# Attention and feed-forward block on one Trainium2 core: a new table of positions for an attention unit, its products with the values in two stretches beside the turn of the maxima

## The chip, the cores and the metric

One core of one Trainium2 chip runs the whole program in one launch. The metric is device time in microseconds (us) of that launch. Beside it stands the span, the time from the first to the last instruction of one profiled execution. An engine is named as in the profile: PE is the matrix engine (TensorE), PEld its weight loads, DVE the vector engine, ACT the scalar engine, POOL is GpSimd, SP issues most of the transfers (DMAs).

## The reference

One layer over x with 2048 tokens of 512 values: a modulated layer norm, attention in 32 heads of 16 values in which each token sees itself and the 255 tokens before it, a second modulated layer norm, and a gated feed-forward of inner size 1792, both added to x.

```
mod = (silu(c) @ w_mod).reshape(1, 6, 1, 512); sa, ca, ga, sb, cb, gb = mod[:, 0..5]
h = layernorm(x) * (1 + ca) + sa
q, k, v = split((h @ wqkv), 32 heads of 16)
scores = where(0 <= i - j < 256, q @ k.T * 16**-0.5, -1e9)
x = x + ga * (softmax(scores) @ v @ wo)
h = layernorm(x) * (1 + cb) + sb
x = x + gb * ((silu(h @ w1) * (h @ w3)) @ w2)
```

## The kernel before, in words

The program has a prologue (modulation, layer norm, the values v of all tokens), an attention stage, and a feed-forward stage that begins while attention ends. The change is in the attention stage.

**Units.** Attention is cut into 32 units u, numbered by a group g of four heads and a block b of 512 tokens (u = 4g + b). A unit has three parts, written by three functions.

- `unit_a` (L442): twelve products `pj` (128x512, L451) make queries and keys of the unit from the normed tokens. ACT cuts the result out of PSUM into three tiles (L457 to L463), POOL takes two differences (`mix`, L469, about 1.29 us each), and SP sends three sets of rows (`rows`, L474, two DMAs each) into the big tile `ring`, where queries and keys of all tokens stand.
- `unit_b` (L491): sixteen products `mx` (L504, up to 128x384) give the scores with queries on the partitions. DVE takes the maximum of each (`top`, L511), joins the sixteen (`parts`, L519 and L520, tile `mr`), PE turns the little tile over (`turn`, L526), ACT cuts it out (`mT`, L531), and SP sends it as extra rows of the queries into `ring` (L535, two DMAs, one for each index a of 0 and 1). So a later product subtracts the maximum by itself.
- `unit_c` (L743): sixteen products `st` (L763) give the scores with keys on the partitions, indexed by a key block j of 0 to 3, by a, and by hh. Each covers the queries of up to three blocks of 128 tokens: for j = 2 and 3 the last of these lie in the next unit's block, so they read the rows that the next unit's turn has sent. A mask or a merge on DVE (L771, L781), the exponential on ACT (L775, L784, L800, L812) and a select on POOL (L791, L808) make the probabilities `pt`, of which nine tiles exist. Then `pv` (L735) multiplies them with the values into the one PSUM tile `po`: for each j four products of 17 columns, each in a 32-column part of the array. A unit's own four calls are for j = 0 to 3; two more are for j = 2 and 3 of the unit before it, whose keys reach into this block. At last ACT copies `po` out (`out`, L828) and SP stores it (L831).

PSUM holds three banks for `mx` and the turn, three for `st`, one for `pj`, one for `po`.

**What sets the order.** Every step is handed to `at` with a position, a number; the steps of all units are sorted by it and given out in that order, and each engine works through its own list in order. Unit u's part c starts at position 8u, its part b at 8(u-2) + ob, its part a at 8(u-3) + oa; the table `X` (L30) gives the offsets within a part. A unit is thus eight positions long, and three units are under way at once. From position 232 (`TS`, three units before the end) on, the steps keep their order, but a planner (`Sched`, L115) puts other work between them: first the projection with `wo` (L1120), then the second norm and the feed-forward. It works from modelled times, so a new table moves its choices too.

Of the kernel before, what the change touches and what calls it, by code (L numbers as in the profile page):

```python
# [26 lines left out]
NEG = -1e30  # L27
SCALE = DH ** -0.5

X = dict(oa=-1.228, ob=1.317, wqk=(-2.382, 3.131, 4.551), pj=(-1.966, -1.918, -1.881, -0.877, -0.359, -0.355,  # L30
         -0.265, 0.076, 1.497, 3.335, 3.917, 4.363), ev=(4.727, 5.775, 5.259), mix=(5.588, 6.021),
         row=(8.681, 8.806, 9.018), mx=(0.546, 0.669, 1.455, 2.0, 2.064, 2.307, 2.929, 2.957, 3.255, 4.081,
         4.688, 5.039, 6.139, 6.215, 6.787, 7.106), tl=(0.31, 0.576, 0.39, 0.716, 0.354, 0.742, 0.497, 1.151,
         0.762, 0.785, 0.491, 0.953, 0.338, 1.726, 1.317, 1.105), mr=(8.575, 8.773, 9.063, 9.269), st=(1.873,
         1.594, -2.503, 2.891, 0.05, 3.409, 2.644, 3.504, 4.618, 4.477, 4.419, 5.916, 5.311, 7.665, 6.691,
         6.671), c=(0.385, 0.805, 2.402, 0.573, 0.759, 1.126), pv=(4.115, 8.948, 9.091, 9.582, 3.792, 4.101),
         o=(9.93, 10.63), job=(-0.855, 2.493, 10.058))
Y = dict(wqk=(0, 4, 5), pj=(0.0, 0.382, 0.764, 1.146, 1.528, 1.91, 2.292, 2.674, 3.056, 3.438, 3.82, 4.202),
         ev=(4.991, 4.614, 4.813), mix=(5.389, 5.444), row=(5.416, 5.471, 6.776), mx=(0.0, 0.5, 1.0, 1.5,
         2.0, 2.5, 3.0, 3.5, 4.0, 4.5, 5.0, 5.5, 6.0, 6.5, 7.0, 7.5), tl=(0.402, 0.402, 0.402, 0.402, 0.402,  # L40
         0.402, 0.402, 0.402, 0.402, 0.402, 0.402, 0.402, 0.402, 0.402, 0.402, 0.402), mr=(8.402, 8.563,
         8.761, 9.49))
# [260 lines left out]
def block_kernel(ctx: ExitStack, tc: tile.TileContext, x, wqk, wv, wo, w13, w2, c, wmod, out):  # L303
# [137 lines left out]

    def unit_a(u, t0, at, y=X):  # L442

# [47 lines left out]
    def unit_b(u, t0, at, y=X):  # L491

        g, b = divmod(u, NB)
        v = {}

        def scores(i):
            qb, a, hh = i // 4, i // 2 % 2, i % 2
            gq = 4 * b + qb
            k0 = max(0, gq - 2)
            n = (gq + 1 - k0) * P  # L500
            if i == 0:
                v["mt"] = a1.tile([P, 2, 2, 4], F32, name="mt", bufs=2)
            v[i] = psA.tile([P, BT], F32, name="mx", bufs=MXB)
            nc.tensor.matmul(v[i][:, :n], queries(NS, a, gq, 1), keys(NS, hh, a, k0, gq + 1 - k0),  # L504
                             start=True, stop=True)
# [226 lines left out]

    held = {}

    def pv(kb, g, pts, qb, c0, nq, first, last):  # L735


        for i in range(4):
            nc.tensor.matmul(po[32 * i:32 * i + DH + 1, qb * P:(qb + nq) * P],  # L739
                             vS[:, kb, 4 * g + i], pts[i // 2][:, i % 2, c0:c0 + nq],  # L740
                             start=first, stop=last, skip_group_check=True)

    def unit_c(u, t0, at):  # L743

        g, b = divmod(u, NB)
        v = {}
# [68 lines left out]
        def values_of(j, uu):  # L815

            kb = 4 * (uu % NB) + j
            pts = [held[uu, j, a] for a in range(2)]
            nq = min(3, NT - kb)
            here = min(nq, 4 - j)  # L820
            if uu == u:
                pv(kb, g, pts, j, 0, here, b == 0 and j == 0, j == 3)
            elif nq > here:
                pv(kb, g, pts, 0, here, nq - here, j == 2, False)

        def out():
            v["os"] = a2.tile([P, BT], F32, name="os", bufs=1)
# [5 lines left out]
        for j in range(4):  # L833
            for a in range(2):
                m, c = mode(j, a), X["c"]
# [68 lines left out]
    for n in range(NU - 4):  # L904
        gate = 0 if n < 8 else 1
        if n >= 3 and n % 4 != 2 and gate == 0 and wog_left:
            i = wog_left.pop(0)
# [29 lines left out]
    last = [o for o in ops if o[0] >= TS]  # L937
# [557 lines left out]
    for b in range(NB):  # L1495
        at_ = us(8 * (NU - NB + b) + X["o"][1]) + 0.1
        o = sch.op("NIL", lambda: None, 0.0, 0.0, [], [("o_dr", b, NQ - 1)])
# [15 lines left out]
    for b in range(NB):  # L1513
        kb, ks = kb_[b], K["os"] + 0.1 * b
# [99 lines left out]
```

## Time and profile before

| | |
|---|---|
| median of three runs | 972.69 us (969.67 to 973.76) |
| span of the profiled execution | 971.3 us |
| PE busy in the span | 942.4 us (97%), 5316 instructions |
| DVE, ACT, POOL busy | 734.9 us (76%), 557.1 us (57%), 538.2 us (55%) |
| attention outputs `os` copied out | first at 109.9 us, last at 488.1 us |

The profile gives no time of its own for the profiled execution beside the span; the median of the runs is 1.4 us above that span. A line of the timeline has the start, the length, the engine, the line of the kernel, the operation, its tiles as out<-in, the shape, and in brackets how long the engine had been idle and what ended that. Matmuls overlap: the length of one is modelled to the end of its pass, and the next one starts before it. An idle time in brackets therefore counts only what lies beyond that modelled end.

### The profile page before, as it was taken

How to read it: one execution, taken by the hardware profiler on the slowest of the kernel's cores; microseconds unless marked ns; L12 is line 12 of the kernel's file. 1: busy time of each engine (PE TensorE's matmuls, PEld its weight loads, DVE VectorE, ACT ScalarE, POOL GpSimd, SP SyncE). 2: the span in 40 equal slices, each digit the busy share in tenths (PEclk: the TensorE clock that was granted, in tenths of full speed). 3: DMA queues.
4: the chain of work that ended last, by engine and by line, in shares of the span. 5: the costliest groups of instructions: out<-in, count | busy, mean ns of one | idle time of the engine just before them, and what ended most of it. 6: DMA issues, size and time to landing. Idle time of an engine off the chain costs nothing.

```text
span 971.3 us, 17150 instructions
## 1 busy us (share of the span) xinstructions
PE 942.4 (97%) x5316; PEld 717.5 (74%) x5316; DVE 734.9 (76%) x2034; ACT 557.1 (57%) x1258; POOL 538.2 (55%) x740
## 2 busy tenths in 40 slices
PE   6999999999999999998998999999999999999998
PEld 3678777777767776775577888888887888888886
DVE  7575889998989998999278686666679766677545
ACT  3333878787878787876578843433456343433330
POOL 8321777787868786865546765337759332222320
PEclk9999999999999999999898999999999999999999
DMA  9521354444544444435795564467654433222102
GB/s 317 170 77 36 134 182 143 144 143 144 176 143 143 144 144 143 133 128 174 211 243 139 194 217 151 142 206 249 194 195 165 141 119 94 63 65 72 44 23 87
DMA packets 80672, 141.65 MB, mean 146 GB/s; under 512 B 9538, under 2 KB 22338, under 8 KB 80580
## 3 DMA queue, kind: packets, MB, share of 16 engines
q1 hardware_dynamic: 79860, 139.50, 44.6%
q10 hardware_dynamic: 720, 1.05, 0.3%
q8 instruction: 42, 0.69, 0.3%
q14 instruction: 50, 0.41, 0.1%
HBM read 85.72 MB, written 34.61 MB: 124 GB/s over the span
## 4 chain that ended last, share of the span: by engine, by line
PE 83%; POOL 5%; DVE 4%; DMA 3%; issue 2%; ACT 2%; SPq 1%; POOLq 0%; DVEq 0%; ACTq 0%
PE st L1384 13%; PE mx L1384 11%; PE pj L451 7%; PE mx L504 7%; PE mx L1478 7%; PE st L763 7%; PE st L1478 7%; PE po L739 6%; PE pj L1384 5%; PE st L671 3%; PE pj L1478 2%; PE mx L1120 2%; POOL pt L791 2%; PE st L1120 2%; POOL qk L469 2%
## 5 line engine op out<-in xcount | busy, mean ns | idle before, releaser
L511 DVE CUSTOM_DVE_ANT_0 junk<-mx,mskq 128x384 bf16<-128x384 f32 (+2 forms) x512 | 256.3, 527 | 28.8 <-PE mx L504 27.2
L504 PE MATMUL mx<-ring 96*128 96x384 f32 (+2 forms) x512 | 154.9, 340 | 6.0 <-DMA ring<-qk 2.4
L763 PE MATMUL st<-ring 100*128 100x384 f32 (+2 forms) x512 | 155.3, 345 | 2.2 <-ACT pt L784 1.2
L791 POOL TENSOR_SCALAR_AFFINE_SELECT pt<-pt 128x256 f32<-128x256 f32 x268 | 109.3, 411 | 63.1 <-ACT pt L784 52.5
L451 PE MATMUL pj<-hT,wq 128*128 128x512 f32 x384 | 136.2, 404 | 1.2 <-DVE wq L440 0.8
L504 PEld LDWEIGHTS mx<-ring 96*128 96x128 f32 x512 | 93.5, 189 | 39.7 <-DVE mt L511 25.8
L784 ACT ACTIVATE pt<-st 128x256 f32<-128x256 f32 x268 | 96.1, 386 | 41.8 <-DVE st L781 33.8
L763 PEld LDWEIGHTS st<-ring 100*128 100x128 f32 x512 | 95.5, 190 | 23.7 <-issue 8.4
L739 PE MATMUL po<-pt,vS 128*17 128x384 f32 (+2 forms) x1408 | 98.6, 398 | 1.7 <-POOL pt L791 1.0
L469 POOL TENSOR_TENSOR qk<-qkr,qk 128x512 fp32r<-128x512 f32 x64 | 83.3, 1302 | 27.6 <-ACT qkr L457 27.4
L976 POOL TENSOR_TENSOR w<-w,w 128x512 fp32r<-128x512 f32 (+2 forms) x36 | 59.8, 1679 | 62.0 <-ACT w L975 44.6
L1428 POOL TENSOR_TENSOR t<-t,t 128x512 f32<-128x512 f32 x28 | 39.7, 1418 | 93.5 <-DVE t L1416 91.7
L781 DVE COPY_PREDICATED st<-later,st 128x128 f32<-128x128 uint8 x268 | 72.2, 291 | 17.4 <-PE st L763 14.5
L451 PEld LDWEIGHTS pj<-hT,wq 128*128 128x128 f32 x384 | 71.4, 190 | 10.2 <-issue 1.7
L739 PEld LDWEIGHTS po<-pt,vS 128*17 128x17 f32 x1408 | 33.5, 98 | 48.4 <-issue 22.4
L1384 PE MATMUL st<-b,w 128*128 128x512 f32 x258 | 64.1, 390 | 0.0
L775 ACT ACTIVATE pt<-st 128x384 f32<-128x384 f32 (+2 forms) x128 | 52.7, 434 | 18.8 <-DVE st L771 12.4
L1416 DVE TENSOR_TENSOR t<-st,t 128x512 f32<-128x512 f32 x52 | 35.7, 686 | 36.4 <-PE st L1384 31.2
L808 POOL TENSOR_SCALAR_AFFINE_SELECT sm<-sm 128x256 f32<-128x256 f32 x109 | 42.1, 409 | 27.9 <-ACT sm L798 25.2
L1456 ACT ACTIVATE wq<-g 128x512 fp32r<-128x512 f32 x28 | 17.8, 634 | 67.5 <-PE st L1478 40.7
L1384 PE MATMUL mx<-b,w 128*128 128x512 f32 x222 | 56.0, 390 | 0.0
L1384 PEld LDWEIGHTS st<-b,w 128*128 128x128 f32 x258 | 48.4, 188 | 10.2
(270 smaller groups left out, 2083.1 us busy)
## 6 DMA issues: line engine op xcount, KB each, us to landing
ring<-qk SPq DMA_DIRECT2D x192, 128.0 KB
o_dr<-os SPq DMA_DIRECT2D x32, 256.0 KB
w<-wsum SPq DMA_DIRECT2D x14, 512.0 KB
w<-w2g SPq DMA_DIRECT2D x14, 512.0 KB
jb<-in_w SPq DMA_DIRECT2D x24, 256.0 KB
wraw<-in_w SPq DMA_DIRECT2D x7, 768.0 KB
w<-wraw SPq DMA_DIRECT2D x14, 384.0 KB
vS<-in_wmod SPq DMA_DIRECT2D x20, 256.0 KB
```

Source lines behind the costliest of these rows:

```text
L451: nc.tensor.matmul(v["ps"], WQ[g][w][:, n // 3], hTp(i, n // 3, b * BT, BT), start=(n == 0), stop=(n == 3 * KC - 1))
L469: nc.gpsimd.tensor_tensor(out=v[n], in0=v["raw"], in1=v[1].bitcast(F32), op=ALU.subtract)
L504: nc.tensor.matmul(v[i][:, :n], queries(NS, a, gq, 1), keys(NS, hh, a, k0, gq + 1 - k0), start=True, stop=True)
L511: nc.vector.tensor_tensor_reduce(out=junk[:, :n], in0=v[i][:, :n], in1=mskq[:, 3 * P - n:], scale=1.0, scalar=-3e38, op0=ALU.add, op1=ALU. ...
L739: nc.tensor.matmul(po[32 * i:32 * i + DH + 1, qb * P:(qb + nq) * P], vS[:, kb, 4 * g + i], pts[i // 2][:, i % 2, c0:c0 + nq], start=first, ...
L763: nc.tensor.matmul(ps[:, :nq], keys(NM, hh, a, kb, 1), queries(NM, a, kb, nq), start=True, stop=not plus)
L781: nc.vector.copy_predicated(ps[:, 0], later, ps[:, 2])
L784: nc.scalar.activation(held[u, j, a][:, hh, :2], v[j, a, hh][:, :2], AF.Exp, scale=SCALE)
L791: nc.gpsimd.affine_select(out=pt[:, :, 2 * m], in_=pt[:, :, 0], **w)
L976: sch.op(eng, lambda: on_eng(eng).tensor_tensor(out=lo(), in0=src(), in1=hi().bitcast(F32), op=ALU.subtract), tt(eng, n), key, kl + kh, kl ...
L1384: nc.tensor.matmul(ps(bk), WT[s, n][w][:, col], BB[t, k][r], start=start and c == 0, stop=stop and c == 5, skip_group_check=True)
L1478: nc.tensor.matmul(ps(bk), tiles[hk + (h,)][:, i * P:(i + 1) * P], w2_of(last, y, f), start=(m == 0), stop=(m == 5))
```

## The change

The table `X` is replaced, which moves nearly every step of a unit. Two small edits let the order of steps change: the tile of maxima is made by whichever `mx` product comes first, and the first product with the values in a block, whichever it is, starts the sum in `po` (with `stop` always set).

```diff
@@ L30
-X = dict(oa=-1.228, ob=1.317, wqk=(-2.382, 3.131, 4.551), pj=(-1.966, -1.918, -1.881, -0.877, -0.359, -0.355,
-         -0.265, 0.076, 1.497, 3.335, 3.917, 4.363), ev=(4.727, 5.775, 5.259), mix=(5.588, 6.021),
-         row=(8.681, 8.806, 9.018), mx=(0.546, 0.669, 1.455, 2.0, 2.064, 2.307, 2.929, 2.957, 3.255, 4.081,
-         4.688, 5.039, 6.139, 6.215, 6.787, 7.106), tl=(0.31, 0.576, 0.39, 0.716, 0.354, 0.742, 0.497, 1.151,
-         0.762, 0.785, 0.491, 0.953, 0.338, 1.726, 1.317, 1.105), mr=(8.575, 8.773, 9.063, 9.269), st=(1.873,
-         1.594, -2.503, 2.891, 0.05, 3.409, 2.644, 3.504, 4.618, 4.477, 4.419, 5.916, 5.311, 7.665, 6.691,
-         6.671), c=(0.385, 0.805, 2.402, 0.573, 0.759, 1.126), pv=(4.115, 8.948, 9.091, 9.582, 3.792, 4.101),
-         o=(9.93, 10.63), job=(-0.855, 2.493, 10.058))
+X = dict(oa=-4.796, ob=-2.251, wqk=(1.186, 6.699, 8.119), pj=(-2.741, -2.421, -2.211, -1.547, -0.122, -0.074,
+         0.522, 1.025, 1.074, 2.472, 2.614, 2.671), ev=(2.692, 5.036, 4.238), mix=(5.574, 6.76), row=(6.587,
+         7.93, 8.329), mx=(4.257, 3.565, 1.99, 2.496, 1.136, 5.297, 5.616, 7.133, 3.18, 8.031, 1.491, 2.403,
+         6.488, 4.019, 2.272, 5.408), tl=(1.032, 0.638, 0.158, 0.51, 0.269, 0.803, 1.089, 0.704, 0.353, 1.162,
+         0.473, 0.456, 0.909, 0.376, 0.547, 1.073), mr=(9.863, 10.174, 10.231, 10.614), st=(-5.114, -3.184,
+         -1.405, -0.284, 1.27, -0.446, 0.145, 0.722, 4.856, 3.979, 1.375, 1.585, 2.957, 2.64, 3.771, 3.671),
+         c=(0.491, 1.492, 2.078, 0.51, 0.82, 3.255), pv=(2.043, 7.743, 8.008, 7.924, 2.306, 2.173), o=(9.93,
+         10.63), job=(-0.855, 2.493, 10.058))
@@ unit_b, scores
-            if i == 0:
+            if "mt" not in v:
                 v["mt"] = a1.tile([P, 2, 2, 4], F32, name="mt", bufs=2)
@@ pv
-    def pv(kb, g, pts, qb, c0, nq, first, last):
+    def pv(kb, g, pts, qb, c0, nq, first):
...
-                             start=first, stop=last, skip_group_check=True)
+                             start=first, stop=True, skip_group_check=True)
@@ unit_c, values_of
+            first = "pv" not in v
             if uu == u:
-                pv(kb, g, pts, j, 0, here, b == 0 and j == 0, j == 3)
+                v["pv"] = True
+                pv(kb, g, pts, j, 0, here, first)
             elif nq > here:
-                pv(kb, g, pts, 0, here, nq - here, j == 2, False)
+                v["pv"] = True
+                pv(kb, g, pts, 0, here, nq - here, first)
```

With the offsets added up, these are the positions in the frame of unit u (its part c starts at 0, the next unit's at 8):

| step | before | after |
|---|---|---|
| first stretch of products with the values | 3.79 (j = 2 of u-1), 4.10 (j = 3 of u-1), 4.12 (j = 0) | 2.04 (j = 0), 2.17 (j = 3 of u-1), 2.31 (j = 2 of u-1) |
| second stretch | 8.95 (j = 1), 9.09 (j = 2), 9.58 (j = 3) | 7.74 (j = 1), 7.92 (j = 3), 8.01 (j = 2) |
| `po` copied out by ACT | 9.93 | 9.93 |
| maxima of u+1: `parts`, turn, rows sent | 1.89, 2.09, 2.59 | -0.39, -0.08, 0.36 |
| first `st` of u that reads those rows (j = 2) | 4.42 | 1.38 |
| queries and keys of u+3: rows sent | 7.45, 7.58, 7.79 | 1.79, 3.13, 3.53 |
| first `mx` of u+3 | 9.86 | 6.89 |
| POOL's side job (`jb`, L880 or L889) | 2.49 | 2.49 |

On PE the turn stood by itself before, between an `mx` and a `pj` or `st`; after, it stands inside the second stretch, behind the products for j = 1. The lines of the kernel after lie up to three further down (the output copy is L831, the store L834, the projection with `wo` L1123).

## Prediction

> **What bounds the kernel now.** I read the page first, then the stretches, then PE's timeline of one unit, then what PE waits for.
>
> ```profile
> span 971.3 us, 17150 instructions
> PE 942.4 (97%) x5316; PEld 717.5 (74%) x5316; DVE 734.9 (76%) x2034; ACT 557.1 (57%) x1258; POOL 538.2 (55%) x740
> PEclk9999999999999999999898999999999999999999
> ```
>
> PE is busy for 97% of the span. The stretches of 50 us say the same of steady attention:
>
> ```profile
> 150.00:200.00 50.00, 49.64 (x371) 36.44 (x371) 46.36 (x196) 40.08 (x114) 39.24 (x73) 1.00 0.45 149
> 350.00:400.00 50.00, 47.87 (x362) 34.86 (x362) 44.10 (x190) 38.70 (x111) 36.01 (x65) 1.00 0.43 139
> ```
>
> The columns are PE, PEld, DVE, ACT, POOL busy, the granted clock, the DMA share and GB/s. PE is idle for 0.4 to 2.1 of 50 us, at full clock; DVE stands at about 90%, ACT at 80%. So a reordering can win only what PE loses between products, and lose as much as its new waits cost. How long a unit is, two copies of `po` say, 27 units apart:
>
> ```profile
> 122.38 0.60 ACT L828 ACTIVATE os<-po 128x512 f32<-128x512 f32 x1 [0.17 <-PE po L739]
> 444.55 0.60 ACT L828 ACTIVATE os<-po 128x512 f32<-128x512 f32 x1 [0.71 <-PE po L739]
> ```
>
> (444.55 - 122.38) / 27 = 11.93 us, so one of its eight positions is worth 1.49 us. Now PE inside one unit:
>
> ```profile
> 250.08 0.34 PE L504 MATMUL mx<-ring 96*128 96x384 f32 x1
> 250.35 1.62 PE L739 MATMUL po<-pt,vS 128*17 128x384 f32 x24
> 251.89 0.44 PE L763 MATMUL st<-ring 100*128 100x384 f32 x1
> 252.17 0.34 PE L504 MATMUL mx<-ring 96*128 96x384 f32 x1
> 252.35 0.34 PE L763 MATMUL st<-ring 100*128 100x384 f32 x1
> 252.53 0.34 PE L504 MATMUL mx<-ring 96*128 96x384 f32 x1
> 253.04 0.28 PE L526 MATMUL mx<-ident,mr 128*32 128x128 f32 x1 [0.18 <-DVE mr L520]
> 253.08 0.47 PE L451 MATMUL pj<-hT,wq 128*128 128x512 f32 x1
> 253.39 0.34 PE L763 MATMUL st<-ring 100*128 100x384 f32 x1
> 253.57 0.40 PE L451 MATMUL pj<-hT,wq 128*128 128x512 f32 x1
> 253.81 0.35 PE L504 MATMUL mx<-ring 96*128 96x384 f32 x1
> ...
> 255.09 0.34 PE L504 MATMUL mx<-ring 96*128 96x384 f32 x1
> 255.36 1.49 PE L739 MATMUL po<-pt,vS 128*17 128x128 f32 x24
> 256.78 0.62 PE L504 MATMUL mx<-ring 96*128 96x384 f32 x2
> 257.23 0.52 PE L763 MATMUL st<-ring 100*128 100x384 f32 x2
> ```
>
> Starts count here, not lengths. A 384-column product takes 0.175 us from start to start (252.17 to 252.35), a `pj` 0.235 (253.57 to 253.81). A product shown as 0.34 long thus hides 0.165 us: a wait shown as 0.18 idle cost 0.34 (252.53 to 253.04 is 0.51, less 0.175). A stretch costs something at its ends: 255.09 to 255.36 is 0.27, or 0.09 over the product; after it, 256.78 to 257.23 is 0.45 for two products, 0.10 over.
>
> **The change part by part.** Numbers and shapes of the attention products stay; two stretches a unit stay two. What changes is what stands beside what.
>
> *(1) The rows of queries and keys, sent earlier.* What PE waits for between 122 and 445 us:
>
> ```profile
> L504 PE MATMUL mx<-ring 96*128 96x384 f32 (+2 forms) x433 | 129.5, 340 | 3.7 <-DMA ring<-qk 2.0 <-DVE st L781 1.3 <-issue 0.2
> L526 PE MATMUL mx<-ident,mr 128*32 128x128 f32 x27 | 7.4, 276 | 0.9 <-DVE mr L520 0.9
> 374.66 0.41 PE L504 MATMUL mx<-ring 96*128 96x384 f32 x1 [1.82 <-DMA ring<-qk]
> ```
>
> The `mx` products have 3.7 us of idle time before them, in about six places, each the first `mx` of a unit (the last row is the largest). With the hidden 0.165 six times this is 4.7 us. Before, the last rows are due at 7.79 and the first `mx` at 9.86: 2.07 positions, 3.1 us. After, 3.53 and 6.89: 3.35 positions, 5.0 us. The largest wait, 1.8 us, is about covered by the 1.9 us gained. On SP the rows now stand behind the store of `os`, which waits for ACT's copy at 1.93, so some slack goes; I count **-4.7 us**, between 0 (a row set late behind that store) and -4.7.
>
> *(2) The turn waits less for `mr`.* The row of L526 has 0.9 us of idle in five places, with the hidden part 0.9 + 5 x 0.165 = 1.7 us. What makes `mr` late:
>
> ```profile
> 251.78 1.00 DVE L519 TENSOR_SCALAR mr<-mt 128x16 fp32r<-128x16 f32 x1
> 240.40 0.17 DVE L519 TENSOR_SCALAR mr<-mt 128x16 fp32r<-128x16 f32 x1
> 251.46 1.28 POOL L880 TENSOR_TENSOR jb<-jb,wqr 128x512 f32<-128x512 f32 x1
> ```
>
> L519 takes 0.17 us, but 1.00 where POOL's gating job (251.46 to 252.74) lies over it, and ends when that ends. After, `parts` is due at -0.39 (7.61 of the unit before) and the job stays at 2.49; POOL's next products, the mixes, come at 0.78. PE also has the j = 1 products between. I count **-1.7 us**, between -1.7 and, if a mix ran into `parts` in every unit, +0.34 x 30 = +10; I take the near end, since 1.2 positions (1.7 us) lie between.
>
> *(3) A drain behind a stretch goes.* 250.35 to 251.89 is 1.54 us for a stretch that an `st` follows; 255.36 to 256.78 is 1.42 for the same three groups with an `mx` behind. In the built program that `st` waits on PE's own semaphore, for `pt` tiles that the stretch frees; 25 `st` directly behind a stretch do so before, none after. 25 x 0.12: **-3.0 us** (0 if the freed tile is merely asked for later).
>
> *(4) The turn inside a stretch.* Alone, it cost little: 253.04 to 253.08 is 0.04, and the `pj` behind it 0.31, 0.08 over its 0.235; 0.12 in all, part of it its own pass. Inside, it uses the 32-column form that the products around it use. I count 0, between -0.12 x 30 = -3.6 and +3.6, and come back to it.
>
> *(5) The rows of the maxima, read sooner.* This is the added wait. Between the turn and the first `st` with j = 2, the built program has before: 257.23 - 253.04 = 4.19 us of PE's work. After: products for j = 3 and 2 (three blocks of 128; the stretch above has six in 1.42 less 0.12, so 0.65), leaving the stretch 0.12 + 0.10, three `pj` (0.71), and eight of `mx` and `st` (1.40), with the turn's 0.12: 3.10 us. Three quarters of the units have such an `st` (the last block of a group has none): 20 in the steady part. When do the rows land?
>
> ```profile
> 253.78 1.41 SPq L535 DMA_DIRECT2D ring<-mT  x2
> GB/s 0 0 0 0 131 0 0 0 0 0 0 0 0 0 0 0 12 53 0 0 0 0 25 41 0 229 393 344 426 360 328 164 131 98 98 344 410 393 426 345
> 313.73 0.27 PE L526 MATMUL mx<-ident,mr 128*32 128x128 f32 x1
> 317.76 0.30 PEld L763 LDWEIGHTS st<-ring 100*128 100x128 f32 x2 [0.24 <-DMA ring<-mT]
> ```
>
> The second row is the DMA rate from 253 to 258 us in slices of 0.125: the two little transfers, issued one behind the other, move in slices 17 and 18 and 23 and 24, so the second (a = 1, which the first `st` needs) has moved by 256.0, 2.96 us after the turn began at 253.04. The last two rows are the one place where an `st` was held by such rows: 317.76 - 313.73 = 4.03 us. Between 2.96 and 4.03 I take 3.35, nearer to the packets, since nowhere else did 4.19 fail. 3.35 - 3.10 = 0.25 us, 20 times: **+5.0 us**; from 0 to (4.03 - 3.10) x 20 = +19. Behind the waiting `st` on PE stand its neighbour, a `pj`, two `mx` and the first stretch; DVE's tops and ACT's exponentials of those wait with them, so the whole unit moves.
>
> *(6) `po` copied out closer to its next use.* Position 1.93 against a first product at 2.04 instead of 3.79. Now ACT comes early and waits (0.17 and 0.71 us in the rows of L828 above). After, the second stretch ends two positions before; ACT's queue ahead of the copy hides it or not. 0, at worst 0.60 x 30 = +18 if it lay open each time; near 0, as ACT has 10 of 50 us free.
>
> *(7) DVE, POOL and ACT work in another order.* Each keeps its instructions in a unit. DVE is the tightest:
>
> ```profile
> PEld mx L504 <- DVE mt L511: 21.4, 44, 0.6
> ```
>
> That is the wait for a free `mx` bank between 100 and 445 us: in weight loads, which run ahead; PE's own row of L504 names no such wait. After, three `mx` stand almost together behind the second stretch, but that stretch gives DVE 1.6 us to empty the banks. 0, between 0 and +21 if every such wait reached PE; near 0, as none does now. On POOL the two mixes (1.29 us each) now stand ahead of a unit's first masks; those are used more than four positions later.
>
> *(8) The tail.* From 445 us on the planner mixes in the projection with `wo`:
>
> ```profile
> 450.00:460.00 10.00, 8.19 (x46) 4.26 (x45) 9.46 (x28) 6.83 (x15) 3.66 (x6) 0.83 0.71 213
> 470.00:480.00 10.00, 8.72 (x66) 4.51 (x64) 2.49 (x7) 4.70 (x11) 6.38 (x9) 0.83 1.05 309
> 454.92 0.92 PE L504 MATMUL mx<-ring 96*128 96x384 f32 x2 [0.96 <-DVE mt L511]
> 455.76 2.75 PE L739 MATMUL po<-pt,vS 128*17 128x384 f32 x24
> 460.76 0.28 PE L526 MATMUL mx<-ident,mr 128*32 128x128 f32 x1 [1.34 <-DVE mr L520]
> ```
>
> PE waits 0.96 and 1.34 us for DVE here, and right behind a stretch takes 2.75 us instead of 1.62 at a clock of 0.83. After, parts a and b end 3.57 positions earlier against part c: fewer `mx` stand beside the last `st`, 48 instead of 24 projection products stand ahead of the last stretch, and the DVE work ahead of the last `parts` is shorter. The two waits and one slow stretch (2.3 + 1.1) may go; the last rows of maxima find less cover (two units, about 0.7 us each). 0.7 x 2 - 3.4 = **-2.0 us**, from -6 to +6.
>
> Sum: -4.7 - 1.7 - 3.0 + 5.0 - 2.0 = -6.4 us on the span of 971.3, so 964.9. The runs' median lies 1.4 us over the span: **966.3 us**.
>
> **The rivals.**
>
> *The rows of the maxima take the place of all that was won (slower).* At 4.03 us from turn to `st`, step 5 costs 19 and the sum is 971.3 - 9.4 + 19 - 2 = 978.9, with 1.4 about 980. Gain and loss without the tail meet at a wait of 9.4 / 20 = 0.47 us, a landing 3.57 us after the turn. For it: the job's 256 KB load now goes out just ahead of the rows, and ACT may be held when the turn ends. Against it: one such wait in 32 units before. Chance 0.22.
>
> *The tail gives it back (no change).* With fewer products to fill it, PE has more gaps there, and the clock falls again: 0.83 over 30 us costs 5.1 us. Without the 2.0 of step 8 that is 971.3 - 4.4 + 5.1 + 1.4 = 973.4, or 971 to 974 with a shorter dip. The Trainium skill, "TensorE: Matmul & The Clock Gate", part 1, says that the clock falls to half after an idle window of about 3.4 us and comes back after a busy one. The trace agrees in kind (2.75 us for a stretch at a clock of 0.83), but the idle time ahead of it, 0.96 us, is far shorter than that window. Chance 0.25.
>
> *Each entry to and exit from the 32-column form drains PE (faster still).* If the turn alone paid as a stretch does at its ends, 0.09 + 0.12 + 0.10 = 0.31 us, its place inside saves 30 x 0.31 = 9 us: 957. Against it stands the 0.12 of step 4. The Trainium skill, "TensorEngine Tiling (Array Packing)", Key Properties, says that changing the tiling mode drains the engine, which would make this the rule; the turn's own rows show a third of it. Chance 0.08.
>
> That the change does not do what it says is no case here: the built program has the turn behind the first four products of a second stretch in all units that the table places.
>
> **How the numbers follow.** My forecast, faster by about 6 us, has 0.45, with its own range 960 to 967.8; slower 0.22; no change 0.25; faster still 0.08. A measurement of this kernel can tell 0.5%, 4.9 us, from no change. So faster 0.45 + 0.08 = 0.53, same 0.25, slower 0.22. The range leaves out the ends of both outer cases: 956 to 980.
>
> **What would show it.** Right: hardly any idle of `mx` on `ring<-qk` left; the turn never behind `mr`; L519 always 0.17 us; stretch to next product 1.42 us throughout; new idle before `st` by `ring<-mT`, about 0.25 us in 20 units; units near 11.7 us. Wrong: `st` idle there of 0.5 us or more; first stretches behind ACT's copy; a granted clock under 0.83 between 440 and 490 us, or a last copy of `po` after 488 us.

## The result, and the profile after

| | before | after |
|---|---|---|
| median of the runs | 973.23 us (969.67 to 977.51) | 986.47 us (984.03 to 989.49) |
| span of the profiled execution | 971.3 us | 983.6 us |

The ratio is 1.0132, 95% interval 1.0096 to 1.0169: slower by 13 us, where 6 us faster was forecast. First the page of the changed kernel, in the same three lines.

```profile
span 983.6 us, 17203 instructions
...
PE 946.0 (96%) x5316; PEld 719.1 (73%) x5316; DVE 731.5 (74%) x2034; ACT 554.8 (56%) x1258; POOL 536.5 (55%) x740
...
PEclk9999999999999999999998999999999999999999
```

PE's busy time is 3.6 us longer, the span 12.3. So PE stands idle for about 9 us more, but the page does not say where. The copies of `po` that measured a unit before (ACT, now L831), and the last of them:

```profile
127.08 0.60 ACT L831 ACTIVATE os<-po 128x512 f32<-128x512 f32 x1
...
450.93 0.59 ACT L831 ACTIVATE os<-po 128x512 f32<-128x512 f32 x1
...
493.87 0.60 ACT L831 ACTIVATE os<-po 128x512 f32<-128x512 f32 x1 [3.34 <-PE po L739]
```

(450.93 - 127.08) / 27 = 11.99 us for 11.93. The first of these three copies is 4.7 us late (127.08 for 122.38) and the last of all 5.8 (493.87 for 488.1), but a copy is no fair mark any more: the new table does other work ahead of it. A fair mark is PE's work itself. I give every product of PE the median start-to-start time of its shape in the kernel before, add these up in order, and compare the moments at which the same sum is reached. The table shows how much later than before each kernel is (us); inside a unit the curve swings by 1.5 us either way, because the order differs.

| time in the kernel before, us | 99 | 158 | 215 | 335 | 395 | 468 | 503 | 525 | 560 | 577 | 654 | 738 | 960 |
|---|---|---|---|---|---|---|---|---|---|---|---|---|---|
| after | 0.0 | -1.0 | 2.7 | 2.8 | 2.5 | 2.5 | 4.1 | 8.7 | 7.8 | 9.6 | 9.4 | 12.5 | 12.5 |
| e1, new table to unit 27, then the old | 0.1 | -0.4 | 2.6 | 3.8 | 2.9 | 11.4 | 10.1 | 10.0 | 11.3 | 11.3 | 11.3 | 11.2 | 11.2 |
| e4, planner refitted | 1.1 | 0.6 | 4.1 | 3.4 | 2.7 | 3.1 | 0.2 | 1.8 | 1.7 | 1.7 | 1.8 | 2.1 | 1.8 |
| e9, one number of the planner | 0.8 | -0.2 | 2.7 | 2.8 | 2.0 | 1.1 | 2.1 | 2.4 | 3.3 | 3.3 | 3.3 | 3.3 | 3.3 |
| e13, old table, rows and job earlier | -0.1 | -0.7 | -0.8 | -3.9 | -5.2 | -7.4 | -6.0 | -5.5 | -5.4 | -5.4 | -5.4 | -5.4 | -5.4 |

Up to 468 us, all of steady attention, the change loses 2.5 us. The other 10 come behind it, while the planner mixes projection, second norm and feed-forward. What PE does there (timeline of the kernel after, then of before):

```profile
493.66 1.65 PE L1123 MATMUL st<-wo,x1b 128*128 128x512 f32 x6
497.15 8.78 PE L1123 MATMUL st<-wo,x1b 128*128 128x512 f32 x30 [1.84 <-ACT x1b L1103]
...
511.68 3.42 PE L1123 MATMUL mx<-wo,o 128*128 128x512 f32 x12 [1.44 <-DVE o L1106]
515.53 1.89 PE L1123 MATMUL mx<-wo,o 128*128 128x512 f32 x7 [0.43 <-DVE o L1106]
...
528.17 0.47 PE L1258 MATMUL st<-ident,wqr 128*128 128x128 f32 x1 [2.40 <-ACT t L1262]
...
531.03 1.22 PE L1123 MATMUL pj<-wo,o 128*128 128x512 f32 x2 [1.76 <-ACT t L1262]
```

```profile
493.51 8.32 PE L1120 MATMUL st<-wo,x1b 128*128 128x512 f32 x36
501.67 2.88 PE L1120 MATMUL pj<-wo,x1b 128*128 128x512 f32 x12
...
521.46 2.93 PE L1120 MATMUL st<-wo,o 128*128 128x512 f32 x6 [2.75 <-ACT t L1259]
```

Both start block 1's projection at 493.5 to 493.7. Before, 48 products run through; after, PE has six and then waits for ACT's cut of the next operand, later for DVE's split of the next block and twice for ACT's modulation. The mean clock is not what differs: from 440 to 545 us the granted clock was 0.92 in both kernels, while PE was busy for 97.0 us before and 91.5 after. The feed-forward adds the rest, waits for the splits of weights, 3.7 us in two places (PE's waits from 545 to 760 us; in the kernel before the profile shows none from 530 to 760):

```profile
PE st L1387 <- DVE w L979: 2.2, 1, 2.2
PE st L1387 <- DVE o L979: 1.5, 1, 1.5
```

Inside steady attention the stretches of 50 us look alike:

```profile
150.00:200.00 50.00, 48.44 (x361) 34.99 (x361) 44.80 (x189) 38.49 (x110) 37.03 (x69) 1.00 0.43 141
350.00:400.00 50.00, 49.23 (x367) 35.90 (x366) 44.69 (x194) 38.97 (x111) 37.79 (x70) 1.00 0.44 144
```

What PE waits for between the two copies, 127 to 451 us:

```profile
PE st L763 <- ACT wq L436: 1.6, 6, 0.3
PE mx L504 <- DMA jb<-in_w: 1.3, 1, 1.3
PE mx L504 <- DVE mt L511: 1.0, 3, 0.4
PE mx L504 <- DMA ring<-qk: 0.7, 1, 0.7
PE mx L526 <- DVE mr L520: 0.5, 1, 0.5
PE st L763 <- DMA ring<-mT: 0.4, 1, 0.4
```

`ring<-qk` and `mr` are down, as forecast. `ring<-mT` seems harmless with 0.4 us once. Two rows name the wrong cause, though. An `mx` reads no `jb`: its wait of 1.3 us is that of a unit's first `mx`, and in e9 (a run below with the same steady units) the same place stands under `ring<-qk`. And the six `st` put down to `wq`, which no `st` reads, all start 3.42 to 3.51 us after the turn, as the first readers of its rows. Moreover, these are idle times beyond a modelled end, and a gap of up to 0.165 us behind a product stays out of sight. One unit on PE:

```profile
255.23 0.84 PE L739 MATMUL po<-pt,vS 128*17 128x384 f32 x8
256.00 0.28 PE L526 MATMUL mx<-ident,mr 128*32 128x128 f32 x1
256.22 0.84 PE L739 MATMUL po<-pt,vS 128*17 128x128 f32 x16
256.99 0.45 PE L504 MATMUL mx<-ring 96*128 96x384 f32 x1
...
259.04 0.34 PE L504 MATMUL mx<-ring 96*128 96x384 f32 x1
259.44 0.59 PE L763 MATMUL st<-ring 100*128 100x384 f32 x2
...
260.55 1.49 PE L739 MATMUL po<-pt,vS 128*17 128x384 f32 x24
261.97 0.44 PE L763 MATMUL st<-ring 100*128 100x384 f32 x1
```

Two things are to be read from starts. The stretch with the turn in it takes 256.99 - 255.23 = 1.76 us, the one without it 261.97 - 260.55 = 1.42: the turn costs **0.34 us inside**, where it cost 0.12 alone. And from 259.04 to 259.44 an `mx` takes 0.40 us for its 0.175, with no bracket: that `st` is the first to read the turned rows of a = 1.

So I sum what starts show: for every product of the 27 units between those copies, the time to the next start less the shape's own (0.2345 us for `pj`, 0.1755 for 384 columns, 0.65 for three blocks of values, 0.06 for the turn), by what comes next. Two prices would fall to `mx` or to `st` by the order alone, and have a row of their own, the second: the first product behind a stretch takes at least 0.105 us more than its shape (5.7 us in all after, ahead of an `st`; before, ahead of an `mx`, 10.5 us together with the waits of that `mx`), and the `pj` behind the lone turn takes 0.08 more (2.1 us before). In us:

| lost ahead of | before | after | e5 | e6 | e7 | e15 | e13 |
|---|---|---|---|---|---|---|---|
| other `mx` | 2.4 | 5.6 | 7.3 | 9.0 | 12.7 | 14.3 | 2.3 |
| what follows the first product behind a stretch or a lone turn | 12.6 | 5.7 | 5.7 | 5.2 | 5.3 | 5.3 | 8.3 |
| the first `st` on turned rows | 0.3 | 5.8 | 0.7 | 14.8 | 0.8 | 0.7 | 0.3 |
| other `st` | 3.6 | 3.4 | 2.1 | 5.3 | 6.1 | 10.3 | 3.1 |
| `pj` | 1.1 | 1.0 | 1.1 | 8.6 | 8.3 | 3.1 | 1.0 |
| stretches, at their beginning | 5.6 | 5.0 | 5.2 | 5.0 | 5.0 | 5.2 | 5.6 |
| stretches, inside and at their end, and the turn | 13.4 | 14.7 | 16.2 | 8.0 | 8.8 | 8.7 | 13.3 |
| sum | 39.0 | 41.1 | 38.4 | 56.0 | 47.0 | 47.5 | 34.0 |

### The profile page after: what moved, and what is told of

The parts are those of the page before. It is cut to its first block, busy times and chain, and to the rows that moved or that the text cites. A ratio compares the mean times of both kernels' runs of the same rounds, so it can differ in the third digit from the quotient of the medians.

```text
span 983.6 us, 17203 instructions
## 1 busy us (share of the span) xinstructions
PE 946.0 (96%) x5316; PEld 719.1 (73%) x5316; DVE 731.5 (74%) x2034; ACT 554.8 (56%) x1258; POOL 536.5 (55%) x740
## 3 DMA queue, kind: packets, MB, share of 16 engines
q10 hardware_dynamic: 720, 1.05, 0.3%
## 4 chain that ended last, share of the span: by engine, by line
PE 82%; DVE 7%; POOL 3%; DMA 3%; ACT 2%; issue 1%; SPq 1%; POOLq 0%; ACTq 0%; DVEq 0%
PE st L1387 11%; PE mx L1387 11%; PE st L763 8%; PE mx L504 8%; PE pj L451 7%; PE po L739 7%; PE st L1481 7%; PE mx L1481 7%; PE pj L1387 4%; PE st L671 3%; PE pj L1481 2%; PE mx L1123 2%; POOL pt L791 1%; PE mx L590 1%; DVE junk L511 1%
## 5 line engine op out<-in xcount | busy, mean ns | idle before, releaser
L763 PE MATMUL st<-ring 100*128 100x384 f32 (+2 forms) x512 | 147.1, 346 | 5.8 <-ACT wq L436 1.6
L451 PE MATMUL pj<-hT,wq 128*128 128x512 f32 x384 | 142.4, 398 | 0.8 <-DVE wq L440 0.8
L763 PEld LDWEIGHTS st<-ring 100*128 100x128 f32 x512 | 92.2, 190 | 31.7 <-ACT pt L784 7.8
L739 PE MATMUL po<-pt,vS 128*17 128x128 f32 (+2 forms) x1408 | 97.3, 391 | 0.1
L1387 PE MATMUL st<-b,w 128*128 128x512 f32 x264 | 66.3, 391 | 2.3 <-DVE w L979 2.2
L775 ACT ACTIVATE pt<-st 128x384 f32<-128x384 f32 (+2 forms) x128 | 54.5, 433 | 13.3 <-DVE st L771 11.6
L739 PEld LDWEIGHTS po<-pt,vS 128*17 128x17 f32 x1408 | 31.5, 97 | 34.3 <-issue 19.5
L1419 DVE TENSOR_TENSOR t<-st,t 128x512 f32<-128x512 f32 x47 | 32.3, 687 | 31.2 <-PE st L1387 27.6
L978 ACT ACTIVATE w<-w 128x512 fp32r<-128x512 f32 (+2 forms) x56 | 42.0, 784 | 20.6 <-DMA w<-wraw 15.6
L1387 PE MATMUL mx<-b,w 128*128 128x512 f32 x216 | 53.1, 390 | 0.0
```

The source lines that it names most:

```text
L451: nc.tensor.matmul(v["ps"], WQ[g][w][:, n // 3], hTp(i, n // 3, b * BT, BT), start=(n == 0), stop=(n == 3 * KC - 1))
L763: nc.tensor.matmul(ps[:, :nq], keys(NM, hh, a, kb, 1), queries(NM, a, kb, nq), start=True, stop=not plus)
L1387: nc.tensor.matmul(ps(bk), WT[s, n][w][:, col], BB[t, k][r], start=start and c == 0, stop=stop and c == 5, skip_group_check=True)
```

## The experiments

My theory after the result: two separate losses. Behind attention the planner deals its work in a worse order, because its constants were fitted to the old positions: its own modelled end, from position 232 on, is 530.7 us with the new table and 516.5 with the old. In the units, the turn's place and the rows of the maxima eat what steps 1 to 3 win. Rivals: the steady units leave the loss behind; the last units' new positions lose it however the rest is dealt; the turn's place costs nothing. All kernels here compute the whole reference. Each ratio is to the kernel before, run beside it.

| run | us | ratio, 95% interval |
|---|---|---|
| e1 new table, then old | 982.55 | 1.0084 (1.0062 to 1.0105) |
| e2 turn ahead of the stretch | 1013.13 | 1.0380 (1.0347 to 1.0414) |
| e3 e2, then old | 1001.19 | 1.0271 (1.0243 to 1.0298) |
| e4 planner refitted | 974.44 | 1.0005 (0.9990 to 1.0020) |
| e5 e4, a = 0 read first | 969.69 | 0.9971 (0.9952 to 0.9990) |
| e6 e4, turn behind | 990.17 | 1.0178 (1.0153 to 1.0204) |
| e7 e5 and e6 | 980.74 | 1.0077 (1.0056 to 1.0097) |
| e8 before, part a new | 1074.76 | 1.1052 (1.1006 to 1.1097) |
| e9 one number of the planner | 977.07 | 1.0044 (1.0025 to 1.0063) |
| e10 before, rows earlier | 976.31 | 1.0025 (1.0011 to 1.0038) |
| e11 before, `mx` first | 977.69 | 1.0042 (1.0024 to 1.0060) |
| e12 e10 and e11 | 975.50 | 1.0020 (1.0008 to 1.0032) |
| e13 e10, job's load earlier | 968.27 | 0.9945 (0.9926 to 0.9964) |
| e14 e13 and e11 | 972.55 | 0.9989 (0.9976 to 1.0002) |
| e15 e7, cut later | 980.63 | 1.0081 (1.0060 to 1.0102) |
| e16 the two code edits alone | 971.81 | 1.0005 (0.9992 to 1.0019) |

### Where the 10 us behind attention come from: e1, e4, e9

e1 (X1 is the new table, X the old one; parts a and b take X1 up to unit 28):

```diff
-        unit_c(u, 8 * u, at)
+        unit_c(u, 8 * u, at, X1 if u < 28 else X)
```

> The new table for part c of units 0 to 27 and parts a and b of units up to 28, the old table for the rest, so that all positions from 232 on, and with them the planner's order, are those of the kernel before. Theory 1 (the steady units come out even, and the 12 us are lost behind them, where the planner deals the projection and the second norm between the new positions): the time is that of the kernel before within 3 us, 970 to 976. Theory 2 (the steady units leave the loss behind, by data that land later): the time stays near the changed kernel, 982 to 987.

982.55 us, near the second theory; but the table of equal work shows neither. Up to 395 us e1 runs like the changed kernel (2.9 us late), from 468 us on it loses nothing (11.4, then 11.2): the steady units leave no loss behind. The 8.5 us lie between, at the units where the tables meet, a seam that neither kernel has. As a time the run says nothing; its trace rules out the first rival.

e4 (nearly all constants of the planner, also which engine splits some of the weights; a few of them shown):

```diff
-K = dict(..., os=0.09, ol=(-29.26, -4.358, -61.448, -4.772), pe=(1.308, 32.004, -0.229, 9.552), n=(1, 1, 2, 2),
+K = dict(..., os=3.722, ol=(-75.264, -16.912, -104.909, -47.219), pe=(5.137, 157.144, 3.141, -105.858), n=(1, 1, 3, 2),
```

> The changed kernel with its new table throughout and other constants K for the planner: keys and engines of the projection, second norm and feed-forward, fitted to the new positions on the planner's own modelled end (512.5 us from position 232 on, against 530.7 with the constants as they were, and 516.5 for the kernel before). Theory 1 (the loss is the planner's order, dealt with constants that belong to the old positions): most of the 12 us come back, 969 to 977. Rival (the new positions of the last units lose it however the rest is dealt, since fewer products stand beside the last ones): 982 to 988.

974.44 us: 12 of the 13 come back, with the new table in every unit. Three us late in steady attention, 0.2 at 503 us, 1.8 at the end.

e9:

```diff
-         -2.126, -37.597), pe=(1.308, 32.004, -0.229, 9.552), o=(-92.491, -1.503, 76.848, -7.065),
+         -2.126, -37.597), pe=(-3.7, 32.004, -0.229, 9.552), o=(-92.491, -1.503, 76.848, -7.065),
```

> The changed kernel with a single number of the planner's constants altered: the first entry of pe, the key of the loads of block 0's attention outputs, from 1.308 to -3.7 (the planner's own modelled end goes from 530.7 to 516.3). Theory 1 (the 12 us are an order that the planner falls into by its old constants, not something that the new positions cost): most of them come back by this one number, 972 to 978. Rival (the refit won by doing the whole transition better, and the order around block 0 is no part of the loss): 982 to 988.

977.07 us: one key, of the loads of block 0's outputs, gives back 9.4 us. Two windows of the kernel after, then the same of e9 (columns as before: PE, PEld, DVE, ACT, POOL busy, granted clock, DMA share, GB/s):

```profile
490.00:500.00 10.00, 8.16 (x48) 5.25 (x47) 5.29 (x16) 4.97 (x12) 4.92 (x4) 0.87 0.88 230
...
510.00:520.00 10.00, 8.01 (x34) 5.78 (x33) 7.84 (x8) 7.15 (x12) 7.81 (x5) 1.00 1.02 266
```

```profile
490.00:500.00 10.00, 10.00 (x63) 7.39 (x62) 6.75 (x18) 6.47 (x14) 7.43 (x6) 1.00 0.79 215
...
510.00:520.00 10.00, 9.55 (x48) 7.66 (x46) 6.80 (x7) 7.38 (x13) 7.70 (x5) 1.00 1.06 268
```

PE is full again in the first window and nearly so in the second. With fewer waits the granted clock from 440 to 545 us is higher too, 0.95 in e4 and e9 for 0.92, by my estimate some 3 us of what comes back (105 us times 0.03). So most of the loss is an order that the old constants and the new positions make together, and not a price of the positions. Which of the many moved loads is the decisive one was not tried.

### The turn's place: e2, e3

e2 (offsets of parts, turn, cut and rows):

```diff
-mr=(9.863, 10.174, 10.231, 10.614)
+mr=(9.5, 9.96, 10.02, 10.4)
```

> The new table with one line of it moved: parts at 9.5, turn at 9.96, cut at 10.02, rows at 10.4, so that the turn stands by itself between two products ahead of the second stretch instead of inside it. Theory 1 (inside the stretch the turn costs 0.34 us where it cost 0.12 alone): a unit is shorter by about 0.22 us, the 27 steady units by 6 us, and the time is 980 to 982, if the planner's order stays as long as it is. Rival (the place of the turn costs nothing, the units are as long for another engine's sake): units of the same length within 0.05 us, the time 985 to 988.

1013.13 us, a plain miss. PE's waits from 150 to 430 us:

```profile
PE mx L526 <- DVE mr L520: 19.0, 22, 1.3
```

19.0 us in 22 turns is 0.86 each, with the hidden 0.165 about 1.0 us; by starts, 27.8 us ahead of the turns of the 27 units. The units grow by less, 12.71 us from copy to copy of `po` for 11.99, since the stretch is whole again and the rows of the maxima come in time: 19 of the 27 us between the two medians. The rest lies behind attention, in the planner's order, and says nothing of the turn. DVE's maxima end only while the stretch runs. So the place inside the stretch hides a wait of about 1.0 us and charges 0.22 for it; the two could not be told apart by moving the turn forward. e3 is e2 with the seam of e1 behind it:

> Both edits of the two runs above: the new table with the turn ahead of the stretch for the steady units, the old table from position 232 on. Theory 1 (two separate losses): the gains add, 973 less 6 is 967, below both kernels, from 964 to 970. If the turn's place costs nothing: 973, from 970 to 976. If the loss comes from the steady units: 980 or more.

1001.19 us, 29.2 us late by equal work: 19.4 in the units up to 395 us, 9.0 at the seam, almost nothing behind it. It repeats e1 and e2.

### The rows of the maxima: e5, e6, e7, e15

All four stand on e4 and change units 0 to 27 alone.

e5 (the pairs j = 2, a = 1 and j = 3, a = 0 change places):

```diff
-         -1.405, -0.284, 1.27, -0.446, 0.145, 0.722, 4.856, 3.979, 1.375, 1.585, 2.957, 2.64, 3.771, 3.671),
+         -1.405, -0.284, 1.27, -0.446, 0.145, 0.722, 4.856, 3.979, 2.957, 2.64, 1.375, 1.585, 3.771, 3.671),
```

> On the kernel with refitted constants (974.4 us), in units 0 to 27 alone: the two pairs of st products j = 2, a = 1 and j = 3, a = 0 change places, so that the first st behind the turn reads the rows of a = 0, which land 2.55 us after the turn, and not those of a = 1, which land 3.3 us after it. Theory 1 (19 to 20 of the 27 units lose about 0.29 us at that st, 5.6 us in all, mostly hidden in the modelled end of the product before): 968 to 970. Rival (these gaps are something else, the st wait for a bank): 973 to 976.

969.69 us, as expected, and below the kernel before. The gap is gone, 258.15 to 258.33:

```profile
258.15 0.34 PE L512 MATMUL mx<-ring 96*128 96x384 f32 x1
258.33 0.51 PE L771 MATMUL st<-ring 100*128 100x384 f32 x2
```

The row of turned rows in the table falls from 5.8 to 0.7 us. So step 5's wait was there, and the list of waits showed little of it: 0.4 us under its own name, and 1.6 us under `wq`, of which one place in six is left in e5.

e6:

```diff
-mr=(9.863, 10.174, 10.231, 10.614)
+mr=(9.863, 10.27, 10.29, 10.614)
```

> On the kernel with refitted constants (974.4 us), in units 0 to 27 alone: the turn stands directly behind the second stretch instead of inside it (offset 10.27 for 10.174), nothing else moved. The stretch is then 1.42 us instead of 1.76 with the turn, and the turn comes 0.65 us later against what follows 0.22 to 0.34 us earlier. Theory 1: the turn's own cost falls from 0.34 to about 0.12 us (less 6 us in 27 units), but the first st that reads its rows waits 0.87 us longer in 20 units (17 us more): 974.4 - 6 + 17 = 985, from 981 to 990. Rival 1 (the rows wait is no wait for rows): 967 to 970. Rival 2 (neither matters): 973 to 976.

990.17 us. Now the wait comes out into the open (150 to 430 us), and the first rival falls:

```profile
PE st L771 <- DMA ring<-mT: 9.5, 15, 0.8
```

Against the column of the kernel after, whose steady units e4 shares, the turn and the stretches' ends cost 6.7 us less, near the 6 that I had set. The rows cost 9 us more, not 17, and `pj` 7.6 us more, which I had not foreseen.

e7 (both edits):

> Both edits of the two runs above together. Theory 1: the turn costs 6 us less, the first st reads rows that landed 0.75 us earlier, so of the wait of 0.29 + 0.87 us about 0.3 to 0.4 us stay in 20 units; 974.4 - 6 - 5.6 + 7 = 970, from 966 to 972, below the kernel before. If the turn needs 0.34 us wherever it stands: 975 to 978.

980.74 us, a miss by 9. The rows wait is gone (0.8 us) and the turn nearly as cheap as in e6, yet `pj` and the other `mx` and `st` lose about 16.6 us more than in e5. ACT's waits, e7 and then e15:

```profile
ACT mT L539 <- PE mx L534: 30.0, 23, 2.3
```

```profile
ACT mT L539 <- PE mx L534: 19.7, 22, 3.9
```

ACT stands for the turn, with the copy behind it that frees the one `pj` bank. e15 puts that copy ahead:

```diff
-mr=(9.863, 10.27, 10.29, 10.614)
+mr=(9.863, 10.27, 10.5, 10.614)
```

> The run with the turn behind the stretch and a = 0 first (980.7 us), with one more offset: ACT's cut of the turned tile at 10.5 for 10.29, so that ACT's copy of a pj result (it frees the one pj bank) stands ahead of it and not behind it. Theory 1 (that run gained 9 us at the turn and lost them because ACT stood waiting for the turn, 30 us against 12, with that copy behind, so that pj products lost 7 us): the excess ahead of pj falls from 8.3 to about 1 us, and the time to 970 to 975. Rival (the loss is in the order of DVE and of the rows): 978 to 982.

980.63 us, the time of the rival: `pj` loses 3.1 us for 8.3, as theory 1 wanted, but other `st` and `mx` lose as much more. The copy was one wait in a row of them. Why a turn 0.65 us later lengthens a unit by 0.3 us, when PE has become cheaper, stays open.

### Steps 1 and 3 by themselves: e8, e10 to e14

e8:

```diff
-X = dict(oa=-1.228, ob=1.317, wqk=(-2.382, 3.131, 4.551), pj=(-1.966, ...), ev=..., mix=..., row=...
+X = dict(oa=-4.796, ob=1.317, wqk=(1.186, 6.699, 8.119), pj=(-2.741, ...), ev=..., mix=..., row=...
```

> The kernel before with one part of the change alone: part a (the offsets oa, wqk, pj, ev, mix, row) from the new table, parts b and c and the planner's constants as before. The rows of queries and keys go out 4 to 6 positions earlier against the first mx. Theory 1 (the mx that opens a unit lost 3.7 us shown as idle and up to 7 us in start to start on rows that had not landed): 973.8 less 4 to 7, 967 to 970. Rival (the rows then stand ahead of the rows of the maxima on SP and wait there for POOL's mixes, or the waits pass to another wait at once): 973 to 977.

1074.76 us, 100 off. From 150 to 430 us PE and ACT wait for:

```profile
PE st L764 <- ACT pt L785: 17.6, 26, 1.0
```

```profile
ACT os L829 <- PE po L740: 40.1, 19, 3.6
ACT qkr L458 <- PE pj L452: 19.5, 18, 1.1
```

ACT's cuts of `pj` now stand where its exponentials were due, wait for PE there, and PE's `st` wait for the exponentials. That is read from these rows, not tried by itself. Part a cannot move alone, so e10 moves the rows only:

```diff
-         row=(8.681, 8.806, 9.018)
+         row=(7.581, 7.706, 7.918)
```

> The kernel before with the three row offsets 1.1 positions smaller (7.581, 7.706, 7.918) and nothing else moved. Theory 1 (step 1: the mx that opens a unit waits 1.8 us twice and less in other places for rows of queries and keys; all but the largest wait go with 1.6 us gained): 973 less 3 to 5, 968 to 970. Rival (as in the run that moved all of part a: what waits on SP behind the rows, here the side job's load, is late in its turn): 973 to 978.

976.31 us, the rival's side. PE waits for `ring<-qk` only once more (0.3 us), but the stretches wait for POOL (PE's waits from 122 to 445 us, POOL's from 150 to 430; then SP's queue in e10 and in before):

```profile
PE po L739 <- POOL pt L791: 8.5, 14, 1.0
```

```profile
POOL jb L889 <- DMA jb<-in_w: 11.1, 9, 2.8
...
POOL jb L880 <- DMA jb<-in_w: 5.9, 3, 3.5
```

```profile
201.40 3.89 SPq L474 DMA_DIRECT2D ring<-qk  x6
205.33 0.58 SPq L893 DMA_DIRECT2D jb<-in_w  x1
```

```profile
208.58 0.39 SPq L893 DMA_DIRECT2D jb<-in_w  x1
209.88 3.90 SPq L474 DMA_DIRECT2D ring<-qk  x6
```

The rows passed the side job's load on SP. POOL's job waits for the load, the selects wait behind the job, the values behind the selects. e13 sends that load earlier too:

```diff
-job=(-0.855, 2.493, 10.058)
+job=(-1.9, 2.493, 10.058)
```

> The kernel before with the rows of queries and keys 1.1 positions earlier, as in the run of the rows alone (976.3 us), and with the load of the side job 1.05 positions earlier too (job offset -0.855 to -1.9), so that it stays ahead of the rows on SP as it was. Theory 1 (the rows alone lost because the job's load came behind them, POOL waited 20 to 40 us for it and the selects behind the job held the stretches for 8.8 us): the stretches wait less than 2 us for POOL's selects, and step 1's gain of 3 to 5 us shows: 968 to 971. Rival (rows sent earlier gain nothing in the old table, since the mx then wait for DVE): 972 to 976.

968.27 us, as expected: 0.9945 of before, the lowest time and ratio of all runs, though the interval of e5 overlaps. PE's waits, 122 to 445 us:

```profile
PE mx L526 <- DVE mr L520: 0.8, 5, 0.2
...
PE po L739 <- POOL pt L791: 0.3, 1, 0.3
```

Two more rows have 0.4 us each. The loss behind a stretch's first product, where a unit's first `mx` stands, falls from 10.5 to 6.2 us (12.6 to 8.3 in the table), and nothing else rises. e11 is step 3 in the old table:

```diff
-         1.594, -2.503, 2.891, 0.05, 3.409, 2.644, 3.504, 4.618, 4.477, 4.419, 5.916, 5.311, 7.665, 6.691,
+         1.868, -2.503, 2.891, 0.05, 3.409, 2.644, 3.504, 4.618, 4.477, 4.419, 5.916, 5.311, 7.665, 6.691,
```

> The kernel before with one st offset moved (the second of j = 0, 1.594 to 1.868), so that an mx and not an st stands directly behind the second stretch. Theory 1 (step 3: the st waits 0.12 us for PE's own stretch to end, 25 times): less 3 us, 969 to 971. Rival (the freed tile is only asked for later, or the mx meets a bank that DVE has not yet emptied): 972 to 976.

977.69 us, slower. The first `mx` of a unit comes 0.2 us sooner and meets rows that have not landed (100 to 445 us; 2.4 us in three places before):

```profile
PE mx L504 <- DMA ring<-qk: 7.2, 8, 1.7
```

> Both edits of the two runs above on the kernel before. Theory 1 (the gains of steps 1 and 3 are real and add, and the change lost them by the turn's place and the rows of the maxima): 973 less 6 to 8, 965 to 967, the fastest of all. Rival (one takes the other's place): no less than 969.

975.50 us: e10's loss, with 7.1 us of stretches behind POOL's selects.

> The run above with the mx ahead of the st behind the second stretch (step 3). Theory 1 (step 3 lost 4 us alone only because the mx then met rows that had not landed, 7.2 us of waits for 2.4): with the rows early and the job's load in its place, 3 us less than the run above, 965 to 968. Rival (the mx that comes earlier meets another wait, a bank that DVE holds): within 1 us of the run above or slower.

972.55 us: 4 us slower than e13. With both known obstacles away the swap still costs, by the same sums 2.2 us ahead of `pj` and 1.7 ahead of other `st`, against 1.2 less ahead of other `mx` and behind a stretch's first product.

The swap could not win what step 3 promised either, for the 0.12 us do not lie behind the stretch. They lie inside it, ahead of the products for j = 3, whose loads of weights wait for POOL's select. First POOL and PE's loads in the kernel before, in the stretch of 250.35 that the prediction shows, then the loads in e14:

```profile
250.61 0.89 POOL L791 TENSOR_SCALAR_AFFINE_SELECT pt<-pt 128x256 f32<-128x256 f32 x2
251.55 0.13 PEld L739 LDWEIGHTS po<-pt,vS 128*17 128x17 f32 x8 [0.42 <-POOL pt L791]
```

```profile
265.55 0.13 PEld L739 LDWEIGHTS po<-pt,vS 128*17 128x17 f32 x8 [0.43 <-POOL pt L791]
```

POOL's select ends at 251.50, and the last eight products start at 251.55, 0.33 us after the four ahead of them, which take 0.216 where nothing waits. By starts this wait stands in 20 of the 27 second stretches, 3.6 us in the kernel before and 3.2 in e14, whether an `st` or an `mx` comes behind; in the kernel after it stands in none. By the table, the last scores for j = 3 now come 4.2 positions ahead of their values instead of 1.9; that this is what took the wait away was not tried by itself.

### The code edits: e16

> The changed kernel with the old table put back: only the two small edits of the change stand (the tile of maxima made by whichever mx comes first; the first product with the values in a block starts the sum, stop always set). All theories expect no difference from the kernel before, within 1.5 us: 972 to 975. If stop on every product cost PE an ending of the sum each time, 54 stretches of 24 products would show it: more than 976.

971.81 us, 1.0005 of before: all of the change is in the table.

## Why the prediction was wrong, point by point

- **(8) The tail, -2.0, from -6 to +6. This step failed**: +10 us (2.5 late at 468 us, 12.5 at the end), 12 of the 20 us between forecast and measurement. I read the tail as a stage with three waits of its own and asked which of them would go. I had written that a new table moves the planner's choices, and saw that 48 for 24 products now stand ahead of the last stretch, but counted that as filling. In the trace ACT now waits 3.34 us for that stretch before the last copy of `po` (493.87), block 1's operand is cut behind that copy and three passes of the second norm, and PE runs dry ahead of 497, 512, 516, 528 and 531 us; that the first of these draws the others after it was not tried by itself. e4 and e9 show that the planner's order is the cause: 12.0 and 9.4 us come back with no position of an attention step changed. The rival "the tail gives it back" had the place, but priced it by a slow clock alone, at 5.1 us, and the mean clock did not change. Of the signs set down for the tail, the last copy after 488 us came; so did a clock under 0.83, 0.67 from 460 to 470 us, but from 450 to 480 us it had been 0.83 before.
- **(4) The turn inside the stretch, 0, from -3.6 to +3.6. Failed**: 0.34 us for 0.12, 27 times 0.22 is +6.0 us. I took it that the turn uses the form of the products around it. It does not: a stretch ends before it and a new one begins behind it (0.12 and 0.21 us by the rows of 255.23 to 256.99). The faster rival had the right rule with the wrong sign, that each entry and exit is paid; the turn inside pays one more of each instead of saving its own.
- **(1) Queries and keys sent earlier, -4.7.** Right in kind, short in size. The waits behind a stretch's first product are gone (10.5 to 5.7 us, which is its bare price). But a unit's first `mx`, which now stands ahead of the stretch, still waits for its rows in two units, 0.7 and 1.3 us of idle or 2.3 by starts: 2.5 us won. e13, which sends the rows 1.1 positions earlier with the job's load kept ahead, gains 5.5 us.
- **(2) `mr`, -1.7.** Right in kind: 1.9 us were lost ahead of the turn before, 0.7 in two turns after, so 1.2 us won. What I missed is that the stretch gives the turn this cover: e2 shows 1.0 us a turn without it.
- **(3) The drain, -3.0.** The figure came true by luck, the mechanism was wrong. All whole stretches take 1.42 us after, as forecast, and 3.6 us are won there. But what went was no drain behind the stretch and no wait of the `st` on PE's own semaphore: it was the wait for POOL's select inside it, as e14's rows show. I had set the two ends of the stretch of 250.35 against those of another and not looked at the starts between. The seven short first stretches, eight products of 384 columns, won another 2.0 us (1.05 to 1.08 us before, 0.77 after); they too had a wait inside, and no term of mine has it.
- **(5) The rows of the maxima, +5.0.** Right: 5.5 us, by 0.20 to 0.24 us in twelve units and 0.40 to 0.67 in seven. In the unit shown the cover was 3.20 us for 3.10 (the turn's price went into it), the first `st` began 3.44 us after the turn for 3.35, and most of the wait lay under modelled ends.
- **(6)** 0: right. **(7)** 0, up to +21: near 0. Other `st` lose 3.4 us for 3.6; three waits of `mx` for DVE's maxima are new, 1.0 us of idle or 1.5 by starts.

Steps 1 to 7 together cost 2.1 us by the sums of starts and 2.5 by equal work, with its swing; I had -4.4. Step 4's 6.0 us is most of that; what steps 1, 2 and 7 fell short of, the unforeseen part of step 3 about makes up for. The rival that ended slower named the rows of the maxima; they are 5.5 of the 19 us it gave them, and not what decided.

## What to carry to other kernels

Where a planner or a list order stands behind the stage that you change, its output is a term of the sum like any other, and a jagged one: here one key moved 9 us. Fit its constants to the new positions before judging the positions. An early transfer must be followed in its queue: what it passes is late (e10), and moving that as well brought the largest gain (e13). And waits of 0.2 us do not show as idle; they are found by starts, from product to product: a stretch taken as a whole hid where its wait stood (step 3), and sums by what comes next change when the order does.

## What the runs showed of the hardware

- A 32-column product of the full array between products in four 32-column parts costs 0.34 us, nearly three times its price between 128-column products: 0.12 us at the end of the first stretch, 0.21 from its start to the next one's. The Trainium skill, "TensorEngine Tiling (Array Packing)", Key Properties, says that changing the tiling mode drains the engine; the rows agree, and by it the turn is in another mode than the stretch. Whether its shape sets it apart or its being a transpose was not tried.
- The rows of the maxima land at nearly fixed times after the turn, above all in the new table: by the last semaphore update of their DMAs 2.54 to 2.62 us for a = 0 in 30 of the 32 units after, 3.27 to 3.38 for a = 1 in all; before, 2.54 to 2.96 and, but for one unit, 3.27 to 3.54. Reading a = 0 first is worth 0.7 us of cover for nothing (e5).
